# A tuned transformer block on one core: a new order of work from the first input tile to the end of K

## The chip, the cores and the metric

The kernel runs on one core of a Trainium2 chip. The metric is the device time of one execution in microseconds (us). A ratio in this document is the mean time of one kernel's fast runs over the mean of the other's fast runs of the same rounds; it is therefore not quite the ratio of the medians quoted beside it. The span of a profile is about 2 us shorter than the time of the same run.

Much of what follows is read from *start times* of instructions and *landing times* of transfers in the trace, where a landing is the last of the sixteen completion marks that a transfer leaves.

Terms: TensorE does the matmuls, VectorE, ScalarE and GpSimd the other arithmetic. Matmuls write to PSUM here ("psum" in the profile); copying from there to the working memory ("arena") is an *eviction*. A *k-tile* is 128 of the 1152 rows over which a matmul sums; a *K pair* is two groups of 128 columns of K for one batch; an *hk* or *scaled tile* is a k-tile of K's input. Line numbers differ by kernel: L788 and L797 of before are L790 and L800 of the changed kernel.

Two quantities recur:

- the **start**: the moment at which the first K matmul begins;
- the **rest**: from the first K matmul to the start of the last matmul of the program. TensorE is dense there, so this is TensorE's own time with its few waits.

## The reference, cut to what matters

```python
B, N, D = 2, 256, 1152                                   # 512 tokens: four tiles of 128, two per batch
mod = (silu(c) @ w_mod).reshape(B, 6, 1, D)
shift_a, scale_a, gate_a, shift_m, scale_m, gate_m = ...
h   = layernorm(x) * (1 + scale_a) + shift_a
qkv = (h @ wqkv).reshape(B, N, 3, 2, D // 2)
a   = softmax(q @ k.T * Dh**-0.5) @ v @ wo
x   = x + gate_a * a
m   = gelu((layernorm(x) * (1 + scale_m) + shift_m) @ w_fc1) @ w_fc2
return x + gate_m * m
```

Only the first part matters here: the layer norm of four tiles, the scale (1152 x 1152 weights times two columns), the shift (as many weights) and K. The kernel computes K from the *scaled* normalised tokens without the shift: the shift adds the same number to all scores of a query, and softmax drops it. So K can begin before the shift weights have arrived.

## The kernel before: the parts in question

A small scheduler in the kernel orders the work. The code is condensed here; "..." and "cut" mark what is left out. TensorE's order is the program's; VectorE's and ScalarE's first instructions are listed by name. Loads are issued in the order written:

```python
KC = 5                                                   # k-tiles of the first group
for b in range(2):
    dma(X[:, 2*b:2*b+2, :], xv[b], ...)                  # two tiles of tokens per load
for (ka, kb) in ((0, KC), (KC, KT)):                     # KT = 9
    for k0 in range(0, KT, 3):                           # scale columns of this group, in three pieces
        dma(WSC[:, k0:k0+3, ka*P:kb*P], ...)
    for kt in range(ka, kb):
        dma(WK[:, kt, :], ...)                           # K weights, one k-tile each
# ... shift weights WSH (3 pieces), Q weights, and the rest follow
```

The start. "xn" is a normalised tile, "hk" a scaled k-tile of K's input, "sca" the small matmuls (two columns each) that make the scale:

```python
# statistics: tiles 1, 2 on VectorE; tiles 0, 3 on ScalarE:
act(Square, accum -> msq); act(Identity, accum -> mean)
dve(var = mean*mean - msq); dve(var = -var + eps); pool(rstd = var ** -0.5)
# TensorE, in order:
xn_T(1); sca 0..2; xn_T(0); sca 3..5; warm(2); sca 6..8; warm(3)
sc1a(0, KC)                                              # VectorE: scale + 1, PSUM -> SBUF
for kt in range(KC): hk(kt, 0, ...)                      # xn^T times scale
for kt in range(KC):                                     # K, batch 0, k-tile by k-tile
    for i in range(4): k_pair((kt,), i, 0)
    if kt == 1: xn_T(2)                                  # 9 transposes of 128 columns
    if kt == 2: xn_T(3)
k_pair(range(KC), 0, 1)                                  # batch 1, first pair
for kt in range(KT): mod_kt(WSC, kt, 0, ..., (KC, KT))   # second group of the scale: 36 small matmuls
sc1a(KC, KT); hk(...) for the other k-tiles
k_pair(range(KC), 1, 1); k_pair(range(KC), 2, 1)
# ... K over k-tiles KC..8 for both batches (cut)
# shift rows: WSH through TensorE as 2-row matmuls; then the last pair of batch 1
copy SHR <- psum[0:98, 0:CH]
k_pair(range(KT), 3, 1, bank=1)
# 9 transposing matmuls of the shift rows, then proj(WK, 8, ...): 9 matmuls of 512 columns
```

VectorE's list begins `..., bn_ln1_2_0, nvar_ln1_0, veps_ln1_0, xn_1, xn_0, ..., sc1a_0, hk_0_0, xn_2, hk_1_0, xn_3, ...`: the normalised tiles of batch 1 come after the first scaled tile. The end of the kernel: the last store waits for all older ones but one.

## Time and profile before

The first three runs took 247.61, 255.12 and 281.97 us; the last two are over 1.5% above the fastest and count as slow.

| what, profiled run of before | us |
|---|---|
| span / time | 245.2 / 247.2 |
| landings: first two tiles, next two tiles | 4.41, 5.92 |
| landings: three scale pieces of the first group | 8.43, 9.68, 10.93 |
| first K matmul (start) | 12.28 |
| landing of the last shift weights | 28.62 |
| first matmul of 512 columns after K | 32.26 |
| rest (first K matmul to last matmul) | 230.11 |

From the page of before, busy time, then TensorE's share and its granted clock in 40 slices of the span:

```profile
PE 240.2 (98%) x1750; PEld 147.6 (60%) x1760; DVE 98.5 (40%) x201; ACT 63.1 (26%) x127; POOL 20.2 (8%) x34
...
PE   7999999999999999999999999999999999999995
...
PEclk9999999999999999999999999999999999999999
```

TensorE (PE) works in every slice. Time can only be won before its dense part begins, by taking work out of it, or after it. The chain that ended last (start us, length us, what) shows how the dense part begins; its lines "issue", of at most 0.05 us, are left out here and in the chains below:

```profile
2.82 8.11 DMA arena<-in_w_mod_dram
10.97 0.67 PE psum L687 x15
11.66 0.18 DVE arena L788
11.87 0.36 DVE arena L797
12.28 1.92 PE psum L687 x16
14.20 0.50 PE psum L690 x9
14.70 0.87 PE psum L687 x8
15.57 0.50 PE psum L690 x9
```

The third scale piece (w_mod) lands at 10.93, fifteen small matmuls follow, then the scale leaves PSUM (L788), the first tile is scaled (L797), and K begins at 12.28. L690 are transposes: two tiles of nine sit inside K.

### The profile page before, as it was taken

The page shows a single profiled execution, that of the slowest core. Times are in us where ns is not written, and L with a number is a line of the kernel's source. Part 1 is how long each engine was busy: PE and PEld are TensorE (multiplying, and loading weights), DVE is VectorE, ACT ScalarE, POOL GpSimd, SP SyncE. Part 2 cuts the span into 40 slices and gives each one's busy share as a digit, 9 for nine tenths or more (in the row PEclk, how much of TensorE's full clock was granted, in tenths as well). Part 3 has the DMA queues.
Part 4 walks back from the last instruction along what each step waited for, and adds up shares of the span by engine and source line. Part 5 has one row for each costly group of instructions (what it writes and reads, how often), then busy time and mean ns, then how long its engine had stood idle before and what let it go on. Part 6 is the DMA issues. An engine that isn't in the chain of part 4 may idle for free.

```text
span 245.2 us, 4025 instructions
## 1 busy us (share of the span) xinstructions
PE 240.2 (98%) x1750; PEld 147.6 (60%) x1760; DVE 98.5 (40%) x201; ACT 63.1 (26%) x127; POOL 20.2 (8%) x34
## 2 busy tenths in 40 slices
PE   7999999999999999999999999999999999999995
PEld 2588754457666766798544444444556655665675
DVE  3743450456312679869999700000012222111112
ACT  5730340244312305983322233222000000000000
POOL 1300000000011166600000000020000000000000
PEclk9999999999999999999999999999999999999999
DMA  6999999999993999969943589003000000000000
GB/s 236 364 377 392 391 390 407 417 422 404 382 305 112 340 387 391 391 211 402 349 122 111 182 268 357 0 3 96 0 16 19 16 16 20 16 16 16 29 22 19
DMA packets 28844, 51.59 MB, mean 210 GB/s; under 512 B 1559, under 2 KB 15643, under 8 KB 28827
## 3 DMA queue, kind: packets, MB, share of 16 engines
q1 hardware_dynamic: 28384, 50.14, 56.7%
q0 software_dynamic: 416, 1.19, 1.5%
q8 instruction: 14, 0.23, 0.4%
q14 instruction: 3, 0.02, 0.0%
q10 hardware_dynamic: 27, 0.00, 0.0%
HBM read 50.14 MB, written 1.19 MB: 209 GB/s over the span
## 4 chain that ended last, share of the span: by engine, by line
PE 94%; DMA 3%; SPq 1%; DVE 0%; issue 0%
PE psum L687 92%; DMA arena<-in_w_mod_dram 3%; PE psum L690 2%; SPq L668 1%; DVE arena L797 0%; DVE arena L1214 0%; DVE arena L1215 0%; DVE arena L788 0%
## 5 line engine op out<-in xcount | busy, mean ns | idle before, releaser
L687 PE MATMUL psum<-arena 128*128 128x384 bf16 (+12 forms) x1661 | 236.7, 310 | 2.4 <-POOL arena L710 1.4
L687 PEld LDWEIGHTS psum<-arena 128*128 128x128 bf16 (+3 forms) x1671 | 142.2, 97 | 92.5 <-issue 4.6
L1214 DVE TENSOR_TENSOR arena<-psum,arena 128x384 f32<-128x384 f32 (+3 forms) x14 | 7.0, 501 | 68.0 <-PE psum L687 68.0
L1124 ACT ACTIVATE arena<-psum 128x512 bf16<-128x512 f32 (+1 forms) x44 | 22.4, 520 | 42.7 <-PE psum L687 42.7
L684 DVE CAST arena<-psum 128x512 bf16<-128x512 f32 (+4 forms) x22 | 13.8, 633 | 31.7 <-PE psum L687 31.6
L682 ACT ACTIVATE arena<-psum 128x512 bf16<-128x512 f32 (+6 forms) x27 | 14.7, 562 | 35.0 <-PE psum L687 32.4
L1025 DVE SCALAR_TENSOR_TENSOR arena<-arena 128x1152 f32<-128x1152 bf16 x16 | 22.7, 1416 | 0.5
L1092 POOL TENSOR_TENSOR arena<-arena 128x384 f32<-128x384 f32 x12 | 10.9, 911 | 14.0 <-DVE arena L1091 11.8
L668 POOL DMA_DIRECT2D dit_scratch<-arena x3 | 1.8, 610 | 116.7 <-ACT arena L682 59.9
L734 DVE BATCH_NORM_STATS2 arena<-arena 128x6 f32<-128x384 f32 (+1 forms) x18 | 9.5, 549 | 0.0
L1037 DVE CAST arena<-psum 72x32 bf16<-72x32 f32 x1 | 0.2, 188 | 21.2 <-PE psum L687 21.2
L1091 DVE TENSOR_TENSOR arena<-psum,arena 128x384 f32<-128x384 f32 x12 | 6.7, 555 | 3.8 <-PE psum L687 3.8
L1097 ACT ACTIVATE arena<-arena 128x1152 bf16<-128x1152 f32 x4 | 5.3, 1344 | 9.8 <-DVE arena L1096 9.8
L690 PEld LDWEIGHTS psum<-arena 128*128 128x128 bf16 (+1 forms) x89 | 5.8, 98 | 2.4 <-DMA arena<-in_c_dram 0.8
L1215 DVE TENSOR_TENSOR arena<-arena 128x384 bf16<-128x384 f32 (+3 forms) x14 | 7.0, 502 | 0.5
L690 PE MATMUL psum<-arena 128*128 128x128 bf16 (+1 forms) x89 | 7.1, 219 | 0.1
L1114 ACT ACTIVATE arena<-psum,arena 128x128 bf16<-128x128 bf16 x16 | 6.1, 455 | 2.8 <-PE psum L690 2.2
L1111 DVE TENSOR_SCALAR arena<-psum,arena 128x128 bf16<-128x128 bf16 x20 | 5.5, 337 | 1.9 <-PE psum L690 1.9
L955 ACT ACTIVATE arena<-psum,arena 128x256 bf16<-128x256 f32 x8 | 3.7, 469 | 7.3 <-DVE arena L952 4.6
L738 POOL TENSOR_TENSOR arena<-arena 128x1 f32<-128x1 f32 x6 | 3.3, 552 | 7.9 <-DVE arena L737 7.9
L951 DVE TENSOR_REDUCE arena<-psum 128x2 f32<-128x512 f32 x4 | 2.8, 692 | 2.6 <-PE psum L687 2.6
L797 DVE TENSOR_SCALAR arena<-psum,arena 128x256 bf16<-128x256 bf16 x7 | 2.4, 349 | 3.6 <-PE psum L690 2.3
(43 smaller groups left out, 42.9 us busy)
## 6 DMA issues: line engine op xcount, KB each, us to landing
arena<-in_w_mod_dram SPq DMA_DIRECT2D x4, 2592.0 KB, 20.2
arena<-in_w_fc_dram SPq DMA_DIRECT2D x9, 1152.0 KB, 7.3
arena<-in_w_fc_dram SPq DMA_DIRECT2D x4, 2592.0 KB, 16.2
arena<-in_wqkv_dram SPq DMA_DIRECT2D x18, 288.0 KB, 9.9
arena<-in_w_mod_dram SPq DMA_DIRECT2D x3, 864.0 KB, 12.5
arena<-in_wqkv_dram SPq DMA_DIRECT2D x1, 2592.0 KB, 12.1
arena<-in_wo_dram SPq DMA_DIRECT2D x1, 2592.0 KB, 32.8
arena<-in_w_mod_dram SPq DMA_DIRECT2D x3, 480.0 KB, 7.5
```

The costliest lines, as they stand in the source:

```text
L682: act(c_act(n), lambda e: e.activation(out=dst, in_=src, func=ACTF.Copy), [src], [dst], name)
L684: dve(c_dve_psum16(n) if psum16 else c_dve_psum32(n), lambda e: e.tensor_copy(dst, src), [src], [dst], name)
L687: S.instr(lambda e: e.matmul(o, lhsT=l, rhs=r, start=st, stop=sp, **kw), reads=[l, r], writes=[o])
L690: S.instr(lambda e: e.transpose(o, i_, idn), reads=[i_, idn], writes=[o])
L734: dve(550, lambda e, s=s, o=o: e.bn_stats(out=o, in_=s), [s], [o], "bn_%s_%d" % (tag, ci))
L1025: dve(1270, lambda e, w=w, s=s, acc=acc: e.scalar_tensor_tensor(out=acc, in0=w, scalar=s, in1=acc, op0=ALU.mult, op1=ALU.add), [w, s, acc] ...
L1091: dve(550, lambda e, o=o, ga=ga, x1c=x1c: e.tensor_tensor(out=x1c, in0=o, in1=ga, op=ALU.mult), [o, ga], [x1c], "wo_t1_%d_%d" % (t, ci))
L1092: S.op("pool", 930, lambda e, xs=xs, x1c=x1c: e.tensor_tensor(out=x1c, in0=x1c, in1=xs, op=ALU.add), reads=[x1c, xs], writes=[x1c], name=" ...
L1114: act(440, lambda e, o=o, dst=dst, s1=s1, s2=s2: e.activation(out=dst, in_=o, func=ACTF.Identity, scale=s1, bias=s2), [o, s1, s2], [dst], ...
L1124: act(c_act(ntok), lambda e: e.activation(out=dst, in_=o, func=ACTF.Gelu_apprx_tanh), [o], [dst], "gelu_%d_%d" % (f, tok0))
L1214: dve(c_dve_psum32(w), lambda e, o=o, gm=gm, t1=t1: e.tensor_tensor(out=t1, in0=o, in1=gm, op=ALU.mult), [o, gm], [t1], "fc2_t1_%d_%d" % ( ...
L1215: dve(c_dve_32(w), lambda e, t1=t1, x1c=x1c, ost=ost: e.tensor_tensor(out=ost, in0=t1, in1=x1c, op=ALU.add), [t1, x1c], [ost], "fc2_out_%d ...
```

## The change

Its intent: start K earlier and take work out of it. Cut to the core:

```diff
-KC = 5
+KC = 4                                    # scale and K in 4+5 k-tiles
 # statistics on ScalarE: sum first; the small operations go to GpSimd
-            act(Square -> msq); act(Identity -> mean)
-            dve(nvar); dve(veps); pool(rstd)
+            act(Identity -> mean); pool(var = mean*mean - eps); act(Square -> msq)
+            (dve if tag == "ln1_3" else pool)(var = msq - var); pool(rstd)
 # scale accumulates over ones, put into PSUM by an identity matmul
-                mm(ps32(7, ...), W[...], ST[...], kt == 0 and f == fs[0], ...)
+                mm(ps32(7, ...), W[...], ST[...], False, ...)
+        sc_ones(0, KC)
-            dve(tensor_scalar(out=o, in0=m, scalar1=1.0, op0=add))          # sc1a
+            dve(tensor_copy(o, m))
+            s1 = ps32(7, 0, 1) if kt == 0 and b == 0 else SC1A[...]         # first hk reads PSUM
 # both tiles of batch 1 ahead of K
+        xn_T(3, 0, 8)
+        xn_T(2, 0, 8)
+        k_first(0); xn_T(3, 8, 9); xn_T(2, 8, 9); k_first(1); ...
-            if kt == 1: xn_T(2)
-            if kt == 2: xn_T(3)
+        k_pair(range(KC), 0, 1); k_pair(range(KC), 1, 1)
+        sc_ones(KC, KT)                    # then 45 small matmuls of the second group
+        k_pair(range(KC), 2, 1)
 # VectorE: ... aggr_ln1_2, var_ln1_3, veps_ln1_2, xn_3, xn_2, hk_0_0, sc1a_0, hk_1_0, ...
+        S.order_after(by["rstd_ln1_2"], by["rstd_ln1_3"])
 # shift rows between the halves of the last K pair
+        k_pair(range(5), 3, 1, bank=1)
         ... shift rows (now in bank 2) ...
-        k_pair(range(KT), 3, 1, bank=1)
+        k_pair(range(5, KT), 3, 1, bank=1)
 # last store
-                        for o in outs[:-2]: wait
+                        for o in outs[:-4]: wait
```

It also has fewer dummy matmuls at the start, other PSUM banks, and new durations in the scheduler's model, which orders what is not listed.

## The prediction

> **What bounds the kernel.** TensorE. The page gives it 240.2 of 245.2 us busy, and the chain of waits puts 92% of the span on its matmul line. By start times in the timeline, the matmuls run back to back from 12.28 us (first K matmul): 109 ns for 256 columns, 215 for 512; waits in the K stage (12.28 to 31.8 us) add up to about 0.5 us. So the only room is before 12.28 us, in small TensorE work inside the K stage, and in the 2.4 us after the last matmul.
>
> **Before 12.28 us.** The chain is: third scale piece lands (10.93), 15 small matmuls, scale evicted on VectorE (11.66, 0.17), first scaled tile (11.87, 0.35), first K matmul (12.28). 18 transposes of batch 1 sit inside the K stage, 0.50 us per tile.
>
> **What the change does.**
> 1. Scale pieces of 4 k-tiles, not 5: the landings (8.43, 9.68, 10.93) should become about 8.3, 9.4, 10.5: 20% fewer bytes, but four-tile pieces ran at 357 GB/s against 393.
> 2. Ones seeded in PSUM; the first scaled tile reads its scale there: the 0.17 us eviction leaves the chain. The Trainium skill (PSUM — Partial Sum Buffer, The four PSUM rules) describes accumulating onto an identity-matmul seed; no run here shows it yet.
> 3. Statistics move from VectorE to GpSimd, freeing about 0.4 us on VectorE at 7.0 us. Normalised tiles 3 and 2 now precede the first scaled tile, so the chain becomes statistics, reciprocal roots (0.55 us each, GpSimd), normalised tiles (0.57 each), transposes. I estimate tile 2 done near 11.45, the first K matmul near 11.95.
> 4. 16 of 18 transposes leave the K stage: minus 0.89 us. The second scale group has 45 small matmuls, not 36 (27 ns each): plus 0.24; the ones: plus 0.06. That group runs nearer to its data: needed from about 17.4, landing at about 17.2 to 18.3 (estimated from the landings), a wait up to 0.2.
> 5. Shift rows between halves of a K pair: their weights land at 28.62 whatever the K stage does; they would start near 28.2 and reach the last piece near 28.9. Neutral, but needed to keep the gain.
> 6. Tail: the older store's landing (242.40) is past before the last store issues (243.38). Nothing gained; perhaps 0.05 lost.
>
> Sum: 0.33 earlier start + 0.89 - 0.24 - 0.06 + about 0.3 fewer waits = 1.2 us. TensorE stays dense afterwards, so it reaches the end: span about 244.0, fast-state time about 246.1 (before: 247.2 when profiled).
>
> **Shown right or wrong by:** first K matmul near 11.95 (start times); at most two transposes inside the K stage; shift matmuls near 28.2; the first 512-column matmul after them about 1.2 us before 32.26; later matmuls unchanged.
>
> **What would make it wrong.** Fewer dummy matmuls: the Trainium skill (TensorE: Matmul & The Clock Gate, Part 1) says an idle window of about 3.4 us halves the clock; this trace shows 427 ns per 512 columns until about 6 us, 215 after. A relapse near 10 us would cost 1 to 2 us. GpSimd small operations could be slower than the 0.25 us I assume and delay tiles 3 and 2. And scatter: before ran 247.6, 255.1 and 282.0, far more than the effect, so a median of few runs may sit above the fast time; hence the high upper end.
>
> Predicted 246.5 us, 245.0 to 256.0; faster by over 2%: 0.03, within 2%: 0.93, slower by over 2%: 0.04.

## The result, and the profile after

The changed kernel took 246.58, 246.57, 247.01 and 247.00 us (median 246.79), the kernel before 247.61 and 247.29 in its fast runs: ratio 0.9973, interval [0.9949, 0.9997]. That is 0.67 us. Output is correct.

From its page, and the chain that ended last:

```profile
PE 239.7 (98%) x1751; PEld 147.4 (60%) x1761; DVE 97.9 (40%) x199; ACT 63.0 (26%) x126; POOL 21.3 (9%) x37
...
PEclk9999999999999999999999999999999999999999
```

```profile
8.72 0.48 DVE arena L734
9.22 0.21 DVE arena L735
9.48 0.16 DVE arena L745
9.72 0.56 POOL arena L746
10.31 0.59 DVE arena L755
10.94 0.62 PE psum L690 x8
11.60 0.62 PE psum L690 x8
12.22 0.87 PE psum L687 x8
13.09 0.11 PE psum L690 x2
13.20 5.99 PE psum L687 x89
19.19 0.17 DVE arena L790
19.38 0.30 DVE arena L800
19.73 11.79 PE psum L687 x130
31.60 10.74 PE psum L687 x49
```

Two things are new. No transfer of weights stands in front of K any more: it is statistics (L734, L735, L745), a root on GpSimd (L746), a normalised tile (L755) and sixteen transposes. And inside K the chain leaves TensorE at 19.19: the second group's scale is evicted (L790) and its first tile scaled (L800), while TensorE waits. The waits of TensorE's weight loads between 12 and 31 us (us in total, times, longest) say the same; the 0.4 us is at the shift weights. Weight loads overlap the matmuls before them (PEld is busy for 60% of the span, PE for 98%), so the matmuls lose less than these waits: 0.15 and 0.22 us by start times:

```profile
PEld psum L687 <- DMA arena<-in_w_mod_dram: 0.4, 1, 0.4
PEld psum L687 <- DVE arena L800: 0.3, 1, 0.3
```

Between the first K matmul and the first 512-column matmul after it, start times give the following sums. (Both traces lack the record of one 512-column matmul at the end of this stretch, so both sums are 0.215 us too long.)

| TensorE's time in us | before | after |
|---|---|---|
| 144 K matmuls of 256 columns, waits included (109.1 ns each without) | 16.020 | 16.045 |
| transposes of batch 1 | 1.005 | 0.112 |
| second group: small matmuls, ones | 0.959 | 1.239 |
| shift rows, waits included | 1.557 | 1.702 |
| transposing the shift rows | 0.445 | 0.445 |
| sum | 19.986 | 19.543 |

So 0.44 us came from inside, 0.22 from the start (12.28 to 12.05), and the sum of 0.67 is still there at the last matmul (242.39 to 241.72). The tail from the last VectorE operation to the end of the span is 1.95 and 1.96 us.

### The profile page after: what moved, and what is told of

The parts are those of the page before. It is cut to its first block, busy times and chain, and to the rows that moved or that the text cites. A ratio compares the mean times of both kernels' runs of the same rounds, so it can differ in the third digit from the quotient of the medians.

```text
span 244.6 us, 4029 instructions
## 1 busy us (share of the span) xinstructions
PE 239.7 (98%) x1751; PEld 147.4 (60%) x1761; DVE 97.9 (40%) x199; ACT 63.0 (26%) x126; POOL 21.3 (9%) x37
## 4 chain that ended last, share of the span: by engine, by line
PE 95%; DVE 3%; POOL 1%; issue 1%; ACT 0%; DVEq 0%; POOLq 0%
PE psum L687 93%; PE psum L690 2%; DVE arena L734 1%; DVE arena L755 1%; POOL arena L738 0%; POOL arena L746 0%; DVE arena L735 0%; POOL arena L710 0%; DVE arena L800 0%; DVE arena L737 0%; DVE arena L1233 0%; DVE arena L1234 0%; POOL arena L709 0%; ACT arena L723 0%; DVE arena L724 0%
## 5 line engine op out<-in xcount | busy, mean ns | idle before, releaser
L687 PE MATMUL psum<-arena 128*128 128x384 bf16 (+11 forms) x1662 | 236.0, 309 | 2.0 <-POOL arena L710 1.4
L687 PEld LDWEIGHTS psum<-arena 128*128 128x128 bf16 (+2 forms) x1672 | 142.2, 97 | 91.8 <-issue 4.3
L682 ACT ACTIVATE arena<-psum 128x512 bf16<-128x512 f32 (+6 forms) x27 | 15.2, 578 | 38.0 <-PE psum L687 35.5
L1111 POOL TENSOR_TENSOR arena<-arena 128x384 f32<-128x384 f32 x12 | 10.9, 910 | 12.6 <-DVE arena L1110 10.4
L734 DVE BATCH_NORM_STATS2 arena<-arena 128x6 f32<-128x384 f32 (+1 forms) x18 | 9.6, 549 | 0.0
L927 ACT ACTIVATE arena<-arena 128x256 bf16<-128x256 bf16 x6 | 2.5, 495 | 4.0 <-DVE arena L921 4.0
## 6 DMA issues: line engine op xcount, KB each, us to landing
arena<-in_wqkv_dram SPq DMA_DIRECT2D x1, 2592.0 KB, 12.7
```

Source lines behind the costliest of these rows:

```text
L682: act(c_act(n), lambda e: e.activation(out=dst, in_=src, func=ACTF.Copy), [src], [dst], name)
L687: S.instr(lambda e: e.matmul(o, lhsT=l, rhs=r, start=st, stop=sp, **kw), reads=[l, r], writes=[o])
L734: dve(550, lambda e, s=s, o=o: e.bn_stats(out=o, in_=s), [s], [o], "bn_%s_%d" % (tag, ci))
L1111: S.op("pool", 930, lambda e, xs=xs, x1c=x1c: e.tensor_tensor(out=x1c, in0=x1c, in1=xs, op=ALU.add), reads=[x1c, xs], writes=[x1c], name=" ...
```

## The experiments

All kernels gave correct results. Each was timed in turn with the kernel before on its chip. "Tile" is the landing of the first two tiles, "scale" that of the first group's third piece.

| run | tile | scale | start | start - tile | start - scale | rest | ratio to before |
|---|---|---|---|---|---|---|---|
| before | 4.41 | 10.93 | 12.28 | 7.87 | 1.35 | 230.11 | |
| changed | 4.38 | 10.31 | 12.05 | 7.67 | 1.74 | 229.67 | 0.9973 |
| e1 transposes inside | 4.26 | 10.36 | 12.01 | 7.75 | 1.65 | 230.43 | 1.0027 |
| e1b and VectorE's order | 4.77 | 11.04 | 12.43 | 7.66 | 1.39 | 230.43 | 1.0013 |
| e2 five and four | 4.83 | 10.65 | 12.50 | 7.67 | 1.85 | 229.05 | 0.9980 |
| e3 old statistics | 4.78 | 11.15 | 13.10 | 8.32 | 1.95 | 229.53 | 1.0020 |
| e4 no ones | 4.76 | 10.79 | 12.44 | 7.68 | 1.65 | 229.50 | 0.9986 |
| e5 shift rows first | 4.88 | 10.30 | 12.56 | 7.68 | 2.26 | 229.54 | 1.0000 |
| e6 old tail | 4.82 | 10.43 | 12.49 | 7.67 | 2.06 | 229.53 | 0.9991 |
| f1 second scale from PSUM | 4.32 | 10.65 | 11.99 | 7.67 | 1.34 | 229.32 | 0.9975 |
| before again | 4.32 | 10.60 | 11.96 | 7.64 | 1.36 | 230.20 | 0.9993 |
| d1 before, tiles late | 6.35 | 10.69 | 13.60 | 7.25 | 2.91 | 230.12 | 1.0069 |
| d2 changed, tiles late | 6.42 | 10.29 | 14.09 | 7.67 | 3.80 | 229.53 | 1.0047 |
| f3 one root | 4.48 | 10.61 | 12.21 | 7.73 | 1.60 | 230.14 | 1.0007 |
| changed again | 4.82 | 10.55 | 12.50 | 7.68 | 1.95 | 229.53 | 0.9979 |
| g3 five and four, shift later | 4.84 | 10.76 | 12.52 | 7.68 | 1.76 | 229.05 | 0.9968 |
| d3 before, tiles a little late | 4.99 | 11.04 | 12.40 | 7.41 | 1.36 | 230.23 | 1.0015 |

Read the fifth column first. In the changed kernel the start follows the tile's landing at 7.67 or 7.68 us, in nine runs that have its statistics and its order of tiles (changed, e2, e4, e5, e6, f1, d2, changed again, g3), with tiles from 4.32 to 6.42. Where the loads are unchanged the tile lands between 4.26 and 5.00, mostly near 4.3 or near 4.8, differently from run to run for the same order of loads. So the profiled run, with 4.38, had an early landing. The intervals of the ratios are 0.13 to 0.54% to either side, too wide for effects of 0.2 us; the traces carry those. Three runs that count as fast have a lower granted clock than the rest (0.993, 0.992 and 0.993, where others have 0.998 to 1.000): one each of e1 (248.95 us), d1 (249.86) and f3 (249.14). They pull their ratios up; without them these are 1.0010, 1.0055 and 0.9977.

### e1 and e1b: the tiles of batch 1 inside K again

```diff
-        xn_T(3, 0, 8); xn_T(2, 0, 8)                     # e1
+            if kt == 1: xn_T(2)
+            if kt == 2: xn_T(3)
-  ... "xn_3", "xn_2", "hk_0_0", "sc1a_0", "hk_1_0",      # e1b, besides
+  ... "hk_0_0", "sc1a_0", "xn_2", "hk_1_0", "xn_3",
```

> Changed kernel with one part undone: all 18 transposes of batch 1 stand inside the K stage again (after its second and third k-tile), the VectorE order stays. Theory (TensorE is dense, terms add): first K matmul at about 11.86 us (freed by the first scaled tile, 11.80, instead of the transposes, 12.05), 0.89 us more transposes inside, the 0.15 us wait for the shift weights gone: the 512-column matmuls of the last K column group begin near 32.15 us (changed kernel 31.60) and the span is about 0.5 us longer. Rival (the weights' arrival sets the end of the K stage, so anything saved before it is given back): 31.6 us and the same span.

> As the run with the transposes inside, and VectorE's order undone too: first scaled tile ahead of the normalised tiles of batch 1. Theory: the first K matmul comes at about 11.55 us, bound by the landing of the scale columns (10.3) alone; the 0.89 us of transposes are paid inside; the 512-column matmuls begin near 31.85 us, span about 0.25 us longer than the changed kernel. That is, putting both tiles ahead is worth 0.25 us and not 0.9, because it delays the first K matmul by 0.5 us. Rival (the tiles ahead cost nothing at the start, the start is bound by the scale): first K matmul stays at 12.05 and the run is 0.9 us slower than the changed kernel.

Measured: in both the rest is 230.43 us, 0.90 us more than the 229.53 us of the changed order without a wait at the shift weights. The transposes are worth what the theory says, and the rival of e1 falls. The start did not come forward as expected in e1 (12.01 against 11.86); there the small matmuls came late and the scaled tile could begin only at 11.60. In e1b it is 1.39 us behind the scale, about as in before, but by coincidence: TensorE reached the small matmuls of the third scale piece only at 11.41, 0.37 us after the landing (11.04), where in before it began them 0.04 us after. The chain of waits of that run leads back to the second pair of tiles, which landed as late as 7.77 us: VectorE's list takes the first piece of tile 2's statistics (L734) before it normalises tile 0 (L755), whose transposes stand in front of the small matmuls:

```profile
1.22 6.55 DMA arena<-in_x_dram
7.79 0.56 DVE arena L734
8.35 0.49 DVE arena L755
8.89 0.68 PE psum L690 x9
9.57 0.51 PE psum L687 x13
10.08 0.52 PE psum L690 x9
10.66 1.33 PE psum L687 x26
12.02 0.37 DVE arena L800
12.43 1.92 PE psum L687 x16
```

My 11.55 for e1b assumed the early scale landing of 10.3. Neither its theory (bound by the scale) nor its rival (12.05 all the same) is tested by this run.

In time e1b is 0.13% over before and e1 0.27% (0.10% without its run at the lower clock), both intervals reaching 1.

### e2: five and four

```diff
-KC = 4
+KC = 5        # hk of k-tile 4 reads the copied xn^T, as its bank is reused
```

> Changed kernel with the split of scale and K put back to 5+4 k-tiles, all else kept. Theory: in the changed kernel the start is bound by the normalised tiles, not by the scale, so a later scale (landing near 10.9) costs only about 0.17 us at the start (first K matmul 12.2), and the second group then has 36 small matmuls and not 45 (0.24 us less) and 1.09 us of K work, not 0.87, behind it, so the 0.22 us wait for its first scaled tile vanishes: 512-column matmuls near 31.3 us, about 0.3 us faster than the changed kernel. Rival (the smaller first group is what brings the start forward): first K matmul near 12.5 and 0.2 to 0.4 us slower.

Measured: rest 229.05, 0.48 us below 229.53 (0.24 + 0.22 expected). The start was 7.67 us behind the tile, bound by it and not by the scale. The 4+5 split is a loss in this order. Of the weight loads' waits in K two small ones remain; neither is the scaled tile's:

```profile
PEld psum L687 <- issue: 0.5, 2, 0.3
PEld psum L690 <- DVE arena L755: 0.2, 1, 0.2
```

Timed, it is at 0.9980 of before, no better than the changed kernel's 0.9973 and 0.9979: with half a microsecond either way for the landing of the tile, three rounds do not show 0.48 us.

### e3: old statistics

```diff
-  pool(mm); act(Square); pool/dve(var); pool(rstd); rstd_ln1_3 first
+  act(Square); act(Identity); dve(nvar); dve(veps); pool(rstd); rstd_ln1_2 first
```

> Changed kernel with the statistics of tiles 0 and 3 as before (square before sum on ScalarE, two more small operations each on VectorE, tile 2 ahead of tile 3). Theory: the start is bound by the statistics chain, so the second normalised tile ends near 12.1 instead of 11.54 and the first K matmul moves from 12.05 to about 12.6 us; 0.15 us of it comes back at the shift weights; 512-column matmuls near 32.0 us, span 0.4 us longer. Rival (the start is bound by the landing of the scale): first K matmul within 0.1 us of 12.05.

Measured: start 8.32 us behind the tile instead of 7.67, so the statistics part (operations and order of the two tiles together) is worth 0.65 us at the start (0.55 expected), and 0.20% over before in time. With the old statistics the new order loses to before. The rival falls.

### e4: no ones

```diff
-        sc_ones(0, KC); sc_ones(KC, KT)
-            s1 = ps32(7, 0, 1) if kt == 0 and b == 0 else SC1A[...]
+            s1 = SC1A[...]                              # after sc1a adds the 1
```

> Changed kernel without the ones: no seed in PSUM, the scale is evicted with the one added (VectorE), and the first scaled tile reads it from there, as before. Theory: the last transposes (end near 12.05) and not the first scaled tile (11.80) free the first K matmul, so 0.2 us more in front of the scaled tile is nearly hidden: first K matmul 12.05 to 12.1, span within 0.1 us of the changed kernel. Rival (as I predicted, the eviction lay on the chain): first K matmul about 0.2 us later.

Measured: 7.68 us behind the tile, as with the ones; the rest is 0.03 us shorter (one matmul of 28 ns less). The eviction that I had counted as taken off the chain is not on the chain of this kernel.

### e5: shift rows ahead of the last pair

```diff
-        k_pair(range(5), 3, 1, bank=1)
         ... shift rows ...
-        k_pair(range(5, KT), 3, 1, bank=1)
+        k_pair(range(KT), 3, 1, bank=1)
```

> Changed kernel with the shift rows in front of the whole last K pair, in the bank they had before. Theory: they start near 27.5 us and then wait for the last shift weights to land (28.6 in the trace of before, 29.6 in that of the changed kernel), so TensorE stands for 0.2 to 1.2 us, whichever landing this run has; the 512-column matmuls begin 0.1 to 1.0 us later than 31.60. Rival (the place of the shift rows does not matter): same within 0.1 us.

Measured: the rest is 229.54, the same. K began at 12.56 in that run, the shift rows at 27.98, and the last weights landed at 28.92, when they were needed (six of nine k-tiles take 0.98 us). Theory and rival are not told apart by it: the wait would be there with a start at 12.05. The place of the shift rows is an insurance.

### e6: old tail

```diff
-  for o in outs[:-4]: wait        +  for o in outs[:-2]: wait
```

> Changed kernel with the waits around the last store as before. Theory: the waits for the older stores are over before the last tile is ready; from the end of the last VectorE operation to the end of the span 2.0 us in either kernel, within 0.1. Rival (the change of the waits shortens the tail): 0.3 us or more longer.

Measured: from the last VectorE operation to the end of the span 1.94 us, against 1.96 and 2.05 in the two traces of the changed kernel. The waits change nothing.

### f1: second group's first scale from PSUM

```diff
-            s1 = ps32(7, 0, 1) if kt == 0 and b == 0 else SC1A[...]
+            s1 = ps32(7, 2 * kt, 1) if kt in (0, KC) and b == 0 else SC1A[...]
```

> Changed kernel plus one thing: the first scaled tile of the second group reads its scale from PSUM too, ahead of the eviction. Theory: the 0.22 us wait of TensorE at 19.5 us, after the small matmuls of the second group and one K pair, is the eviction (0.17) and hand-over in front of that tile; it falls to 0 to 0.05 and the run is 0.2 us faster than the changed kernel, unless the shift weights, which then are reached earlier, take it back (0.15 us wait there growing to 0.3). Rival (the wait is for weights landing): unchanged.

Measured: rest 229.32, 0.21 us less; the wait after that K pair fell from 216 ns to 25 ns. So the wait was the eviction and hand-over ahead of the first scaled tile, not a landing.

### Before again, and the tiles made late in both kernels

> The kernel before, unchanged, for a second trace and as a control (ratio 1.00). The runs so far show the first input tile landing at either about 4.3 or about 4.8 us, and the changed kernel's first K matmul 7.67 us after it (12.05 or 12.5). Theory: the kernel before is bound there by the third piece of scale instead: first K matmul 1.35 us after that landing, whatever the input tile does, so near 12.3 us also where the tile lands at 4.8; then the changed kernel starts 0.2 us earlier in some runs and 0.2 us later in others. Rival: the kernel before follows the input tile too (12.8 us for a landing at 4.8), and its start is then always later than the changed kernel's.

Measured: ratio 0.9993, the control holds. Its tile landed early (4.32), so it does not answer the question it was run for; but its scale landed at 10.60 and the start came 1.36 us later, at 11.96: 0.1 us *earlier* than the changed kernel's profiled start. Its chain, for comparison with that of the first trace:

```profile
2.70 7.90 DMA arena<-in_w_mod_dram
10.65 0.67 PE psum L687 x15
11.34 0.18 DVE arena L788
11.55 0.36 DVE arena L797
11.96 1.92 PE psum L687 x16
```

```diff
             if b == 0:                                  # d1 in before, d2 in the changed kernel
+                dma(WSC[:, 0:3, 0:KC*P], ...)           # first scale piece ahead of the tiles
             dma(X[:, 2*b:2*b+2, :], xv[b], ...)
```

> The kernel before with the first piece of scale loaded ahead of both input tiles, nothing else: the tiles land about 1.2 us later, the third piece of scale at the same time. Theory (the start is bound by the scale): first K matmul moves by less than 0.3 us from 12.28, time within 0.3 us of before. Rival (bound by the tiles' statistics): later by about 1.2 us.

> The changed kernel with the same swap of loads: the tiles land about 1.0 us later (its piece is smaller), the third piece of scale at the same time. Theory (the change moved the start onto the input tiles' statistics): first K matmul still 7.67 us after the first tile's landing, so about 13.1 to 13.5 us, and the run about 1 us slower than the changed kernel, less what the shift weights' wait gives back (0.15). Rival (bound by the scale): unmoved near 12.1 to 12.5.

Measured: d2 is as the theory says, start 7.67 us behind a tile at 6.42, though the scale had landed at 10.29. d1 is not: the kernel before also moved, by 1.3 us. I had mis-sized the swap (it delayed the tile by 1.9 us, not 1.2), and I had overlooked that before has a chain from the tiles too, through the transposes of batch 0: 7.25 us from tile to start in this run. It is 0.42 us shorter than that of the changed kernel. A smaller delay was needed:

```diff
+                dma(WSC[:, 0:1, 0:KC*P], ...)           # d3: one k-tile of scale ahead of the tiles
```

> The kernel before with a sixth-of-a-megabyte piece of the scale ahead of the input tiles, so that the first tile lands near 4.8 us and the third piece of scale when it did. Theory: the start of the kernel before is the later of two chains, third scale landing plus 1.355 us and first tile landing plus 7.25 us (measured 13.595 with the tile at 6.35), so at 4.8 us the scale still decides: first K matmul 1.355 us after the scale's landing, at 12.0 to 12.3; the changed kernel has 12.5 for such a landing. Rival (it follows the tile): 7.95 us after the tile (the distance in the second trace of before is 7.63), near 12.7.

Measured: with the tile at 4.99 the start is 12.40, 1.36 us behind the scale (11.04), where the rival said 12.7. It was close: the second pair of tiles was late too (7.23), and had the scale been there, TensorE would have reached those small matmuls only 0.06 us sooner. So before's start is the later of two chains, scale + 1.36 and tile + 7.25 to 7.35 (by d1 and d3). For a tile at 4.8 that gives about 12.05 to 12.3 (an estimate from these numbers), where the changed kernel has 12.50.

### f3: one root for both tiles

```diff
-            pool(rstd_2 = var_2 ** -0.5); pool(rstd_3 = var_3 ** -0.5)
+            pool(RSTD[:, 2:4] = MV[:, 2:4, var] ** -0.5)
```

> The changed kernel with the two reciprocal roots of batch 1 taken by one GpSimd operation on two columns. Theory: on the chain from the first tile's landing to the first K matmul, the second root (0.55 to 0.69 us, after the first) goes and the two normalised tiles run back to back, so that distance falls from 7.67 to about 7.53 us; gain 0.14 us, below what the timing resolves. Rival (the root is not on the chain): 7.67.

Measured: 7.73, no gain; this theory falls. The root of two columns took 0.70 us where the first of two single ones took 0.55, so, counted from the landing of the tile, the first normalised tile began 0.22 us later than in the changed kernel and the second still 0.06 us later. The start moved by the same 0.06 us, so the roots are on the chain, but joining them gains nothing. The trace shows something else: TensorE stood in the second group's small matmuls, which took 2.05 us instead of 1.20 because the last piece of their weights landed at 19.18 us:

```profile
PEld psum L687 <- DMA arena<-in_w_mod_dram: 0.8, 1, 0.8
PEld psum L687 <- issue: 0.5, 2, 0.3
```

With the 4+5 split TensorE reaches this group at 17.3 to 17.9 us for starts of 12.0 to 12.6; in nine other traces with that split and both tiles ahead of K (both of the changed kernel, e3, e4, e5, e6, f1, d2 and the last experiment) its last piece landed between 17.49 and 18.48.

### The changed kernel again, and the best of the parts

> The changed kernel, unchanged, on the same chip as the two next to it: more rounds for the size of the gain. Theory: inside the K stage it is 0.59 us shorter than before (19.77 against 19.18 us between the first K matmul and the first whole-width matmul, shift wait taken off), and its start is anything from 0.3 us earlier to 0.5 us later, as the first input tile lands at 4.3 or 4.9 us; so 0.1 to 0.9 us faster, 0.2% on the mean, and the first K matmul 7.67 us after the first tile. Rival (my prediction: start always 0.3 us earlier and 1.2 us in all): 0.45% or more.

Measured: 246.67 us median, ratio 0.9979, interval [0.9966, 0.9993]. Tile at 4.82, start at 12.50. The spans of the two second traces, on different chips, are 245.0 for before and 245.0 for the changed kernel, though the timing has it 0.5 us faster on the mean: one trace each says little of a gain this small. Its chain shows the tile at its head, where the fast trace hid it:

```profile
0.80 4.03 DMA arena<-in_x_dram
4.84 1.26 ACT arena L742 x2
6.13 1.26 ACT arena L744 x2
7.39 1.16 ACT arena L742 x2
8.57 1.26 ACT arena L744 x2
9.92 0.16 DVE arena L745
10.08 0.08 DVE arena L737
10.17 0.56 POOL arena L746
10.75 0.59 DVE arena L755
11.39 0.62 PE psum L690 x8
```

Four passes of 1152 columns on ScalarE (L742, L744), back to back from the landing, take 5 of the 7.67 us.

```diff
 # g3: e2's split, and
-        k_pair(range(5), 3, 1, bank=1)
+        k_pair(range(KT), 3, 1, bank=1)
         ... shift rows ...
-        k_pair(range(5, KT), 3, 1, bank=1)
+        first 4 of the 9 matmuls of proj(WK, 8)
         ... transposing the shift rows ...
-        proj(WK, 8, 17, HK, 0)
+        the other 5
```

> Best of the parts: the changed kernel with the 5+4 split back, and the shift rows moved behind the whole last K pair with four matmuls of the last K column group between them and their transposes. Theory: 0.24 us fewer small matmuls, no wait for the second group's first scaled tile (0.22) or for its landing (up to 0.8 in one run of the 4+5 split), none at the shift weights: 0.5 us faster than the changed kernel on the mean, ratio to before about 0.9960. Rival (the weights' arrival sets the end of the stage): as the changed kernel.

Measured: 246.46 us median (246.19 to 246.72), ratio to before 0.9968, interval [0.9955, 0.9980]; the changed kernel on the same chip ran at 246.62 to 246.85. Rest 229.05, as e2: the later shift rows neither cost nor gained in that run. It is clearly ahead of before; ahead of the changed kernel by 0.28 us on the mean of five runs, with overlapping intervals, and by 0.48 us in the trace's rest.

### Why weights land late in some runs

In every trace a 16 KB read of instructions, taking about 1.1 us, appears near 16 and again near 25 us (15.0 to 17.8 and 23.7 to 26.8), when TensorE has issued its 121st to 138th and its 235th to 257th weight load. In most traces the distance between the first and the last of the sixteen marks of a transfer, steady before, jumps by 0.3 to 1.7 us after it. In the profiled run of the changed kernel two jumps (1.14 to 1.73 at the second group, 1.76 to 2.66 at the shift weights) put the last shift weights at 29.64; TensorE reached them at 29.54. The last experiment moved the reads:

```diff
-        warm(7, "b")
+        60 matmuls of two columns
```

> The changed kernel with seven dummy matmuls of 512 columns replaced by 60 of two columns, so that TensorE has issued 53 more pairs of weight load and matmul by any later point. In all traces so far a 16 KB instruction read of about 1.1 us starts when TensorE has issued its 137th and about its 253rd weight load (15 to 18 us and 24 to 27 us), and the last of the sixteen parts of the next weight pieces lands 0.4 to 1.6 us further behind the first from then on. Theory (the read takes one DMA engine away from the weights): the first read moves to about 11 us and the second to about 20 us, and the jump of the lag moves with them, to the first K weights (11 to 13 us) instead of the second group of scale (16 to 19 us). Rival (the lag jumps because of the 1280-byte rows of the second scale group): the jump stays at the second scale group.

Measured, in a single look: the reads moved to 11.97 and 22.03 us. The spread of the second group's landings stayed at 1.76 throughout, so the rival (row size) falls; the second jump (1.77 to 2.24) moved with the second read, from the second and third shift piece to the first. The first read left almost no mark (1.65 to 1.76), so not every read delays the slowest part. That it takes time from one of the sixteen DMA engines fits all this; which engine is hit in a run is not in the trace and stays open. (The weight-load numbers in the expectation count some other records; 121 to 138 is the recount.) This run also began K 8.22 us behind its tile (5.00), and not 7.67: after the 60 small matmuls and 1.3 us of idling, 512 columns took 427 ns from start to start, and the full clock was granted only at 10.12 us (4.75 to 7.60 in the fourteen other traces that record it); the chain to K went through these slow matmuls. It took 247.73 us, before on the same chip 247.13, one run each, so of unknown state.

## Why the prediction was right or wrong

What it said of the bounds was right: TensorE dense, nothing in the tail, under 2%. The headline of 246.5 us was close to the measured 246.79, but the fast runs of before (247.29, 247.61) lie within 1.2 us of it too, so that shows little. What can be checked is the sum of 1.2 us behind it, and that was wrong: two of its terms failed, the start (1) and the waits (5). The runs gave 0.67 us in the profiled pair and 0.67 and 0.52 us by the two timings (ratios 0.9973 and 0.9979). In the profiled pair the start gave 0.22 of 0.33 us; the waits, put down as a gain of 0.3, were a loss of 0.17 (0.025 in the K matmuls, 0.145 at the shift rows). These two terms are nearly the whole shortfall; over the traces together, the start falls further.

1. **"0.33 earlier start" (its step 3): this step failed.** I carried the landings of one trace over to the other and added durations. The start's own estimate, 11.95, was 0.1 from that run's 12.05, but by luck: that run's tile landed early (4.38), and the scale of the profiled run of before late (10.93). What I did not see is that the change ties the start to the first tile's landing, at 7.67 us, and that this landing moves by half a microsecond between runs, while before is tied to the scale at 1.36 us and has 0.3 to 0.6 us of slack against the tiles (12.28 and 11.96 against an early tile plus 7.25 to 7.35). In the five runs with the changed start and unchanged loads (changed, changed again, e5, e6, f1) the mean start is 12.32; in the two of before, both with an early tile, it is 12.12. So the term is between about +0.3 and -0.5 us by run, and not a gain on the mean of these few traces. Its real use is to let the tiles go ahead.
2. **Scale landing (step 1) and eviction (step 2)**: the landings came at 7.81, 8.87 and 10.31, earlier than I said, and did not matter; e2 and e4 show both off the chain. The ones worked as described in the Trainium skill (PSUM — Partial Sum Buffer, The four PSUM rules): results are correct when small matmuls without the first flag add onto an identity-matmul seed.
3. **Transposes, minus 0.89: right.** 1.005 fell to 0.112, and e1 puts 0.90 back.
4. **Small matmuls, plus 0.24, ones, plus 0.06: right**, 0.28 together.
5. **"About 0.3 fewer waits": failed.** The old waits (0.06 and 0.13 us in front of scaled tiles) went. They were all that could go: I had put the K stage's waits at 0.5 us, but the 144 K matmuls of before hold 0.31 beyond 109.1 ns each, of which about 0.1, at the hand-over to the shift rows, is in both kernels. And with one K pair of 0.87 us and no longer two behind the second group, its first scaled tile came too late: 0.22 us, which f1 and e2 each remove. The prediction counted the small matmuls of the second group and its landing, but not the hand-over behind it: VectorE's eviction began at 19.18, 0.54 us after the last small matmul gave way, and the scaled tile was there at 19.67, when the pair had been over for 0.16 us.
6. **Shift rows, "neutral": right in most runs**, 0.15 us lost in the profiled one, because the landing was 29.64 and not 28.62 "whatever the K stage does". The same applies to the second group: a wait "up to 0.2" was 0 in most runs and 0.84 in one.
7. **Clock**: the granted clock stayed full from 5.4 us on (6.1 in before). The Trainium skill (TensorE: Matmul & The Clock Gate, Part 1) gives 426.7 ns for 512 columns in the throttled state and 215.7 in the full one; the trace's 427 and 215 before and after that moment agree. Its idle window of 3.4 us was not tested: in the profiled run no two matmuls before K began more than 0.57 us apart, so the dummies that were left sufficed.

Together: 0.585 us inside (229.53 against 230.11; the other traces of before, with the tiles late or not, have 230.12 to 230.23), less a wait now and then, less about 0.2 us at the start on the mean of the traces, is 0.4 us, and the timings' intervals (0.2 to 0.8 and 0.1 to 1.3 us) hold it.

## What to carry to other kernels

When work is moved ahead of a dense stage, ask which landing the stage's start now hangs on and how much that landing moves between runs; one trace shows one draw of it. Splitting a group so that it starts sooner also takes away the work that hid the next group's hand-over: count what is left behind the split. And for gains below half a microsecond, measure from a milestone inside the trace (here the first K matmul to the last) and repeat the trace, as the whole time mixes them with the landing of the inputs.

## What the Trainium skill lacked or had wrong

- Runtime: NRT & Kernel Launch, section Instruction fetch mechanics, calls the cost of crossing a 16 KiB boundary "mostly hidden". Fourteen such reads are in the profile of before, 0.9 to 1.2 us each; TensorE did not run dry of instructions in what I looked at, but the spread of weight landings jumped by up to 1.7 us after one (1.13 to 2.73 us in f3, with 0.8 us of waiting). The page does not say that these reads compete with the kernel's transfers.
- DMA: Bandwidth & Descriptors, section Why a DMA increments its semaphore by 16 and not by 1, says that the engines finish independently. The runs agree, and add the size: 0.8 to 3.2 us between first and last mark of one weight piece that landed between 11 and 32 us, so a wait is for the slowest engine.
- No page that I read gives the scatter of the first load: the first 590 KB landed between 4.26 and 5.00 us in the kernels with unchanged loads, and the changed kernel's start followed one for one.
- GPSIMD Engine Reference: I found no cost there for operations on one column. They took 0.18 to 0.58 us, a root (power -0.5) 0.55 to 0.82, and 0.70 on two columns.
- TensorE: Matmul & The Clock Gate, Part 1: it does not say how little activity counts as busy. Here five matmuls of 512 columns, then 60 of two columns (27 ns apart, 1.6 us) and 1.3 us idle, left the array at 427 ns per 512 columns, until the full clock came at 10.12 us.
